# Two weight groups on ScalarE's DMA queue, a third without a throttle, and five groups in the first attention block

## The chip, the cores and the metric

The kernel runs on one core of one Trainium2 chip. Five engines work side by side, each through its own list of instructions in order: TensorE (PE, with its weight loads PEld), VectorE (DVE), ScalarE (ACT), GpSimd (POOL) and SyncE (SP), which here only issues DMAs. A DMA is issued by one engine and carried out by 16 DMA engines. The metric is the device time of one execution in microseconds (us). What is compared is the median of several executions.

## The reference

Causal attention with a decay, then two feed-forward layers, all in float32 with float64 weights:

```
q, k, v: (4, 8, 576, 64)   f: (4, 8, 576)
cum   = cumsum(log(clip(f, 1e-4, 1)))
score = q k^T / 8 + cum[:, None] - cum[None, :]      (masked above the diagonal)
x     = softmax(score) v           -> 2304 tokens of 512
h     = x @ w_in  (512 x 2048);    y = max(0.01 h, h) @ w_out  (2048 x 512)
out   = ((y @ w_a) * (y @ w_b)) @ moe2_w_out         (512 x 1536, twice; 1536 x 512)
```

## The kernel before

**Stages.** Attention runs in blocks `(b, r)`: batch `b`, and of its 576 tokens the first 256 (`r = 0`) or the last 320 (`r = 1`). Eight heads go in four pairs. The first feed-forward layer works on chunks of 256 tokens of x: chunk 0 needs only block (0, 0). The first matmul of chunk 0, `h` at L624, can therefore begin as soon as the last pair of block (0, 0) has given its part of x. From there on the matmuls of the feed-forward layers are woven between those of the later attention blocks, and after attention they run alone.

**One pair of the first block.** q and k are loaded and turned by TensorE (`tqk`), copied to `qn` (ACT) and `kn` (DVE); `s` is the score matmul. GpSimd builds the decay and mask `p` from `cumb`, a row of the cumulative sum broadcast over 128 partitions by a DMA that reads `cum_dram`. VectorE adds `s` to `p` and takes the row minimum (L371), ScalarE exponentiates (L339), VectorE makes the reciprocal `rec`, ScalarE multiplies (L380), TensorE transposes (`pp`), ScalarE copies (`ph`), TensorE multiplies with v (`av`), and x comes out as a high part `xh` (ACT) and a low part `xl` (DVE), which split a float32 in two numbers that TensorE takes at full rate. Two chunks of keys per head pass through this, of 128 and of 256 columns. Many of these carry L76, a wrapper's line, so names tell them apart. Buffers of `p` are two per head of a pair, so that pair 2 waits for the transposes of pair 0.

**Weights.** The weights arrive as float64, and a "group" is 128 columns of w_in and 128 rows of w_out: two DMAs of 512 KB into `raw_a`. There are 16 groups, a_0 to a_15. A conversion takes each to float32 high and low parts: `Abs` on ScalarE (L118), four operations on VectorE (L119, L120, L121, L124), a copy to the high part on ScalarE (L111), and the subtraction for the low part on VectorE (L112). A pair of groups is needed by each of the eight steps of a chunk.

**What sets the order.** A scheduler orders the instructions of each engine ahead of time. Attention's operations carry a priority offset of 300 in the first block, conversions none. `load_next` is called at every ninth step of the first block, and each call also fetches a further group. The fetch of group fi waits for the start of the conversion of group fi - 2 (`behind=begun[fi - 2]`). All loads go through SP in order. The DMAs of all engines share eight completion semaphores in turn (`DMAHW0` to `DMAHW7` in the listings of the program order), so a DMA waits for the landing of the one that had its semaphore before, eight earlier.

Of the kernel before, what the change touches and what calls it, by code (L numbers as in the profile page):

```python
# [13 lines left out]
ALU = mybir.AluOpType  # L14
# [3 lines left out]
P = 128  # L18
# [3 lines left out]
TOP_MIN = 2.0**-15  # L22
TOP_MAX = 122874.0
# [3 lines left out]
def kernel(  # L27
# [30 lines left out]
    wpool = ctx.enter_context(tc.tile_pool(name="wpool", bufs=1))  # L58
# [37 lines left out]
    ORDER = mybir.DependencyInfo(mybir.DependencyClass.NoSync, mybir.DependencyReason.DATA)  # L96
# [9 lines left out]
    def f32(ap):  # L106
        return ap.bitcast(F32)
# [3 lines left out]
        nc.scalar.copy(hi, src)  # L111
        (lo_engine or nc.gpsimd).tensor_tensor(out=lo, in0=src, in1=f32(hi), op=ALU.subtract)  # L112

    def from_double(raw, c):


        top, low, t = raw[:, :, 1], raw[:, :, 0], c.bitcast(F32)
        first = nc.scalar.activation(t, top.bitcast(F32), AF.Abs)  # L118
        nc.vector.tensor_scalar(t, t, TOP_MIN, TOP_MAX, op0=ALU.max, op1=ALU.min)  # L119
        nc.vector.tensor_scalar(c, c, 5, 2, op0=ALU.logical_shift_left, op1=ALU.logical_shift_right)  # L120
        nc.vector.scalar_tensor_tensor(  # L121
            out=c, in0=low, scalar=29, in1=c, op0=ALU.logical_shift_right, op1=ALU.bitwise_or
        )
        nc.vector.scalar_tensor_tensor(  # L124
            out=c, in0=top, scalar=-0x40000000, in1=c, op0=ALU.bitwise_and, op1=ALU.bitwise_or
        )
        return t, first

    begun = []
    SYNC = mybir.DependencyInfo(mybir.DependencyClass.Sync, mybir.DependencyReason.DATA)  # L130

    def fetch_weight(pool, tag, name, *parts, behind=None):

        raw = pool.tile([P, 1024, 2], I32, tag=tag, bufs=1, name=f"raw_{name}")
        for z, src in enumerate(parts):
            view = raw[:, 512 * z : 512 * z + 512, :].rearrange("p n t -> p (n t)")
            if len(src.shape) == 3:
                view = view.rearrange("p (a b) -> p a b", b=2 * P)
            ins = nc.sync.dma_start(view, src)  # L139
            if behind is not None:  # L140
                tc.add_manual_dep(ins.ins, behind.ins.name, SYNC, reason="weights wait for an earlier conversion")
            elif pool is wpool and name == "a_1":
                tc.keep_in_program_order(ins)
        return raw, pool, tag, name

    def convert_weight(tpool, raw, pool, tag, name):

        c = tpool.tile([P, 1024], I32, tag="t", bufs=2, name=f"c_{name}")
        t, first = from_double(raw, c)
        w = pool.tile([P, 2, 1024], F32R, tag=tag, bufs=1, name=f"w_{name}")  # L150
        split(w[:, 0, :], w[:, 1, :], t, nc.vector)
        begun.append(first)
        return w[:, 0, 0:512], w[:, 1, 0:512], w[:, 0, 512:1024], w[:, 1, 512:1024]

    def cols(w, j):

        return w[:, 2 * j * P : 2 * (j + 1) * P].rearrange("(c p) f -> p c f", p=P)

    def rows(w, j):
        return w[j * P : (j + 1) * P, :]  # L160
# [22 lines left out]

    fs = ap_.tile([B * H, S], F32, tag="cumb", bufs=3, name="fs")
    nc.sync.dma_start(fs, f.rearrange("b h s -> (b h) s"))
    nc.vector.tensor_scalar(fs, fs, 0.0001, 1.0, op0=ALU.max, op1=ALU.min)
    nc.scalar.activation(fs, fs, AF.Ln)
    ones = ap_.tile([B * H, S], F32, tag="tk", name="ones")  # L190
    nc.vector.memset(ones, 1.0)
    cum = ap_.tile([B * H, S], F32, tag="cumb", bufs=3, name="cum")
# [23 lines left out]
    def att_scores(b, r, h, st):  # L216
# [15 lines left out]
        if b == 0:  # L232
            if j == 0:

                qn = ap_.tile([P, 384], F32, tag="qhh", bufs=2, name=f"qn_{nm}")
                kn = ap_.tile([P, S], F32, tag="ks", bufs=3, name=f"kn_{nm}")
                xq = ap_.tile([P, 2, 2, 64], F32, tag=("xq", "xq2")[hp % 2], name=f"xq_{nm}")
                full, rest = nk // P, nk % P
                xk = ap_.tile([P, 5, 2, 64], F32, tag=("xk", "xk2")[hp % 2], name=f"xk_{nm}")
                for u in range(2):  # L240
                    nc.sync.dma_start(xq[:, 0:2, u, :], q[b, h + u, q0 : q0 + 2 * P, :].rearrange("(c p) d -> p c d", p=P))
                    if r == 1:
                        nc.sync.dma_start(xk[64:P, 4, u, :], q[b, h + u, q0 + 2 * P : S, :])
                    nc.sync.dma_start(xk[:, :full, u, :], k[b, h + u, : full * P, :].rearrange("(c p) d -> p c d", p=P))
                    if rest:
                        nc.sync.dma_start(xk[:rest, full, u, :], k[b, h + u, full * P : nk, :])
                if first:
                    tqk = ps_y.tile([P, 2, T1], F32, tag="y", bufs=2, name=f"tqk_{nm}")
                    tq = tqk[:, 0, :]
                else:  # L250
                    tq = ps_a.tile([P, 320], F32, tag="ps", bufs=3, name=f"tq_{nm}")
                for c, at, w in ((0, 0, P), (1, P, P), (2, 2 * P, 64))[: 2 + r]:
                    part, sl = (xq[:, c, :, :], slice(0, P)) if c < 2 else (xk[64:P, 4, :, :], slice(64, P))
                    pe_att.transpose(tq[:, at : at + w], part.rearrange("p u d -> p (u d)"), ident[sl, sl])
                act_att.mul(qn[:, :nq], tq[:, :nq], -SCALE)
                for c0, c1 in ((0, 2), (2, 5))[: 1 + r]:
# [163 lines left out]
                yield  # L420

    def evac(hi, lo, src):
        act_att.copy(hi, src)
        return dve_att.tensor_tensor(out=lo, in0=src, in1=f32(hi), op=ALU.subtract)


    def att_values(b, r, h, st):
# [7 lines left out]
        if j == 0:  # L435
            full, rest = nk // P, nk % P
            if b == 0:
                vs = ap_.tile([P, 5, 2, 64], F32, tag=("vs", "vhl")[hp % 2], name=f"vn_{nm}")
            else:
                vs = ap_.tile([P, 5, 2, 64], F32, tag="vs", name=f"vs_{nm}")  # L440
            for u in range(2):
                nc.sync.dma_start(vs[:, :full, u, :], v[b, h + u, : full * P, :].rearrange("(c p) d -> p c d", p=P))
                if rest:
                    nc.sync.dma_start(vs[:rest, full, u, :], v[b, h + u, full * P : nk, :])
            if b == 0:
                vhls[pair] = vs
# [39 lines left out]
        if b == 0:  # L486
# [16 lines left out]
                    if kt == u == 0:  # L503
                        tc.add_manual_dep(made.ins, st["second"].ins.name, SYNC, reason="both heads at once")
            ch, cl = x_chunk(tok0 // T1)
            low = evac(ch[:, hp, :], cl[:, hp, :], av)
            if r == 0:
                dve_held.first = low
            yield
            return  # L510
        av = ps_a.tile([P, 256], F32, tag="ps", bufs=3, name=f"av_{nm}")
# [86 lines left out]
    blocks = [(b, r) for b in range(B) for r in range(2)]  # L598
    wa = {}

    landing = []

    def fetch_a():
        fi = len(landing)
        if fi < NF1:
            landing.append(fetch_weight(wpool, f"w{fi}", f"a_{fi}", cols(w_in, fi), rows(w_out, fi), behind=begun[fi - 2] if fi > 1 else None))

    def load_a(fi):
        if fi == 0:
            fetch_a()  # L610
        wa[fi] = convert_weight(stage, *landing[fi])

    def l1(i, pr):
        ch, cl = x_chunk(i)
# [198 lines left out]
    def load_next():  # L813
        nonlocal loaded
        if loaded < NF1:
            load_a(loaded)
            loaded += 1
            fetch_a()

    for s, _ in enumerate(att_steps(0)):  # L820
        if s == 0:
            fetch_a()
        if s % 9 == 8:
            load_next()
    for engine in (act_att, dve_att, pool_att):
        engine.offset = 0
# [103 lines left out]
```

## Time and profile before

| | |
|---|---|
| median of 3 runs (lowest to highest) | 1086.86 us (1086.01 to 1087.88) |
| the profiled execution | 1085.58 us |
| its span, first to last instruction | 1083.8 us |
| mean granted TensorE clock | 0.987 of full speed |
| busy PE, PEld | 1050.4 us (97%), 943.7 us (87%) |
| busy DVE, ACT, POOL | 588.3 us (54%), 549.2 us (51%), 210.4 us (19%) |
| share of PE in the chain that ended last | 89% |

The profiled execution is 1.78 us longer than its span, and 1.28 us below the median. In the page's table of 40 slices, 27.1 us each, PE is busy 3 tenths of the first slice, 6 of the second and 9 of nearly every later one. The averages hide that the engines have different limits in different stretches: VectorE and ScalarE are busy 5 to 9 tenths in the first half and 1 to 2 tenths at the end.

### The profile page before, as it was taken

To read this page: it belongs to the slowest core of one execution; us is meant where nothing else is said; L and a number is where in the kernel's file an instruction comes from. 1 tells how busy PE (TensorE), PEld (TensorE's weight loads), DVE (VectorE), ACT (ScalarE), POOL (GpSimd) and SP (SyncE) were. 2 spreads that over 40 slices of the span, in tenths; PEclk is the share of its full clock that TensorE was granted. 3 is DMA by queue.
4 is the path that set the end of the run, shared out by engine and by line. 5 is a ranking of instruction groups with operands and counts; after the bars stand their busy time and mean duration, and the time that the engine had idled before them with its cause. 6 is when DMAs were issued, how large, how long until landed. Compare 5 with 4: busy or idle time off the path is not lost.

```text
span 1083.8 us, 19124 instructions
## 1 busy us (share of the span) xinstructions
PE 1050.4 (97%) x6941; PEld 943.7 (87%) x6941; DVE 588.3 (54%) x1314; ACT 549.2 (51%) x1221; POOL 210.4 (19%) x434
## 2 busy tenths in 40 slices
PE   3699999999999999999999999999999999999998
PEld 1378789999999999999999998888888888888897
DVE  5899758878787778666439798112112111212122
ACT  5877778877787878677435554112112111211121
POOL 2623524343244324223000001001002000100000
PEclk9689999999999999999999999999999999999999
DMA  8886245333552244321234761102001000100010
GB/s 237 241 261 188 42 88 100 77 91 66 104 107 63 64 86 107 70 47 42 79 98 158 232 233 31 29 1 78 1 1 45 24 1 1 49 0 1 1 40 20
DMA packets 185726, 86.74 MB, mean 80 GB/s; under 512 B 143840, under 2 KB 173536, under 8 KB 185632
## 3 DMA queue, kind: packets, MB, share of 16 engines
q1 hardware_dynamic: 180736, 80.80, 28.5%
q10 hardware_dynamic: 4896, 4.72, 1.3%
q8 instruction: 55, 0.90, 0.3%
q14 instruction: 39, 0.32, 0.1%
HBM read 75.96 MB, written 9.51 MB: 79 GB/s over the span
## 4 chain that ended last, share of the span: by engine, by line
PE 89%; DMA 4%; issue 2%; ACT 2%; DVE 2%; SPq 1%; POOL 1%; POOLq 0%; ACTq 0%; DVEq 0%
PE ab L722 27%; PE y L653 17%; PE h L624 17%; PE o L745 14%; PE s L76 5%; PE av L76 5%; PE pp L76 4%; DMA raw_a<-in_moe_w_out_dram 1%; DMA cumb<-cum_dram 1%; DMA raw_a<-in_moe_w_in_dram 1%; DMA y_dram<-yo 0%; PE tk L76 0%; ACT p L380 0%; SPq L139 0%; POOL p L361 0%
## 5 line engine op out<-in xcount | busy, mean ns | idle before, releaser
L722 PE MATMUL ab<-yh,w_ab 128*128 128x512 f32 (+1 forms) x960 | 279.6, 367 | 0.0
L624 PE MATMUL h<-xh,w_a 128*128 128x256 f32 x1152 | 227.7, 284 | 0.5 <-ACT hs L636 0.3
L653 PE MATMUL y<-gh,w_a 128*128 128x256 f32 x1152 | 225.4, 282 | 0.0
L722 PEld LDWEIGHTS ab<-yh,w_ab 128*128 128x128 f32 x960 | 174.1, 188 | 30.4
L728 DVE TENSOR_TENSOR p<-ab,p 128x512 f32<-128x512 f32 (+1 forms) x60 | 38.3, 638 | 283.3 <-PE ab L722 283.3
L624 PEld LDWEIGHTS h<-xh,w_a 128*128 128x128 f32 x1152 | 185.6, 190 | 3.9 <-issue 1.3
L653 PEld LDWEIGHTS y<-gh,w_a 128*128 128x128 f32 x1152 | 183.3, 188 | 3.6 <-issue 2.4
L722 PE MATMUL ab<-yl,w_ab 128*128 128x512 f32 (+1 forms) x480 | 176.2, 367 | 0.0
L624 PE MATMUL h<-xl,w_a 128*128 128x256 f32 x576 | 163.6, 284 | 0.0
L653 PE MATMUL y<-gl,w_a 128*128 128x256 f32 x576 | 160.6, 281 | 0.0
L745 PE MATMUL o<-w_c,pph 128*128 128x512 f32 x432 | 142.6, 389 | 0.0
L727 ACT COPY p<-ab 128x512 f32<-128x512 f32 (+1 forms) x60 | 32.7, 544 | 172.7 <-PE ab L722 172.7
L361 POOL TENSOR_SCALAR p<-cumb,ncum_t 128x384 f32<-128x384 f32 (+1 forms) x112 | 82.1, 741 | 144.6 <-PE pp L76 70.2
L624 PEld LDWEIGHTS h<-xl,w_a 128*128 128x128 f32 x576 | 109.5, 190 | 0.3
L653 PEld LDWEIGHTS y<-gl,w_a 128*128 128x128 f32 x576 | 108.3, 188 | 0.7 <-issue 0.4
L722 PEld LDWEIGHTS ab<-yl,w_ab 128*128 128x128 f32 x480 | 90.1, 188 | 15.3
L111 ACT CAST pph<-p 128x512 fp32r<-128x512 f32 (+1 forms) x60 | 34.6, 577 | 128.8 <-DVE p L728 128.5
L745 PEld LDWEIGHTS o<-w_c,pph 128*128 128x128 f32 x432 | 81.1, 188 | 16.6
L112 POOL TENSOR_TENSOR yl<-sy,yh 128x512 fp32r<-128x512 f32 (+1 forms) x16 | 19.9, 1254 | 389.3 <-ACT yh L111 389.2
L339 ACT ACTIVATE p<-p,stat 128x384 f32<-128x384 f32 (+4 forms) x128 | 76.9, 602 | 29.6 <-DVE stat L371 23.9
L745 PE MATMUL o<-w_c,ppl 128*128 128x512 f32 x216 | 84.2, 390 | 0.0
L638 DVE TENSOR_TENSOR gl<-hs,gh 128x512 fp32r<-128x512 f32 x72 | 50.6, 702 | 38.4 <-ACT hs L636 37.8
(143 smaller groups left out, 1695.2 us busy)
## 6 DMA issues: line engine op xcount, KB each, us to landing
cumb<-cum_dram SPq DMA_DIRECT2D x32, 288.0 KB, 4.0
raw_a<-in_moe_w_in_dram SPq DMA_DIRECT2D x16, 512.0 KB, 5.4
raw_a<-in_moe_w_out_dram SPq DMA_DIRECT2D x16, 512.0 KB, 6.5
raw_ab<-in_moe_w_a_dram SPq DMA_DIRECT2D x12, 512.0 KB, 5.2
raw_ab<-in_moe_w_b_dram SPq DMA_DIRECT2D x12, 512.0 KB, 6.7
raw_c<-in_moe_w_out_dram SPq DMA_DIRECT2D x12, 512.0 KB, 5.1
xq<-in_q_dram SPq DMA_DIRECT2D x144, 32.0 KB, 2.0
y_dram<-yo ACTq DMA_DIRECT2D x18, 256.0 KB, 2.8
```

The lines of the kernel that those rows point to most:

```text
L76: return method(*args, **kw)
L111: nc.scalar.copy(hi, src)
L112: (lo_engine or nc.gpsimd).tensor_tensor(out=lo, in0=src, in1=f32(hi), op=ALU.subtract)
L339: act_att.activation(pt, pt, AF.Exp, bias=stat[:, 0, s : s + 1], scale=-1.0, accum_out=stat[:, 1, s : s + 1])
L361: pool_att.tensor_scalar(pt, cumb[:, :n], 1.0, ncum_t[:, t, bh : bh + 1], op0=ALU.mult, op1=ALU.add)
L624: made = nc.tensor.matmul(hps[:, u, :], w[:, c * P : c * P + P], x[:, c, :], start=(n == 0), stop=(n == 3 * ND - 1))
L638: nc.vector.tensor_tensor(out=gl, in0=hs, in1=f32(gh), op=ALU.subtract)
L653: nc.tensor.matmul(o, w[:, d * P : d * P + P], g[:, u, :], start=(fi == 0 and n == 0 and d % 2 == 0), stop=(fi == NF1 - 1 and n == 2 and d ...
L722: nc.tensor.matmul(o[:, :tn], w[:, c * P : c * P + P], y[:, c, :tn], start=(m == 0), stop=(m == 3 * ND - 1))
L727: nc.scalar.copy(p[:, :tn], ab[0][:, :tn])
L728: nc.vector.tensor_tensor(out=p[:, :tn], in0=ab[1][:, :tn], in1=p[:, :tn], op=ALU.mult)
L745: nc.tensor.matmul(o, g[:, t * P : t * P + P], w, start=(fi == 0 and m == 0), stop=(fi == NF2 - 1 and m == 2))
```

## The change

Groups a_0 and a_1 are loaded from ScalarE's queue (`engine=nc.scalar`), the first at the very start. Group a_2 is no longer held behind a conversion. The first loads on SP are put in a fixed order (`in_line`): q and k of the first two pairs, then a_2, then v of the first pair, as far as the calls come in that order. `load_next` is called at steps 0, 5, 9, 26 and 44 of the first block, so five groups belong to it. Groups from a_5 on are held (`held=True`): their `Abs` and their first operation on VectorE come, in the order of their engines, behind the copy `xh` and the subtraction `xl` of the first block's last x. That is an order on the same engine and not a semaphore.

```diff
+    first_x = []
-    def from_double(raw, c):
+    def from_double(raw, c, held):
         first = nc.scalar.activation(t, top.bitcast(F32), AF.Abs)
-        nc.vector.tensor_scalar(t, t, TOP_MIN, TOP_MAX, op0=ALU.max, op1=ALU.min)
+        clamp = nc.vector.tensor_scalar(t, t, TOP_MIN, TOP_MAX, op0=ALU.max, op1=ALU.min)
+        if held:
+            for made, x in zip((first, clamp), first_x):
+                tc.add_manual_dep(made.ins, x.ins.name, ORDER, reason="weights behind the first block's last x")
...
+    line = []
+    def in_line(made, early):
+        if early:
+            if line:
+                tc.add_manual_dep(made.ins, line[-1].ins.name, ORDER, reason="order of the first loads")
+            line.append(made)
...
-            ins = nc.sync.dma_start(view, src)
+            ins = (engine or nc.sync).dma_start(view, src)
+            in_line(ins, early)
             if behind is not None:
                 tc.add_manual_dep(ins.ins, behind.ins.name, SYNC, reason="weights wait for an earlier conversion")
-            elif pool is wpool and name == "a_1":
-                tc.keep_in_program_order(ins)
...
+    landing = []
+    def fetch_a():
+        fi = len(landing)
+        if fi < NF1:
+            landing.append(
+                fetch_weight(
+                    wpool, f"w{fi}", f"a_{fi}", cols(w_in, fi), rows(w_out, fi),
+                    behind=begun[fi - 2] if fi > 2 else None, engine=nc.scalar if fi < 2 else None, early=fi == 2,
+                )
+            )
+    fetch_a()
     fs = ap_.tile([B * H, S], F32, tag="cumb", bufs=3, name="fs")
     nc.sync.dma_start(fs, f.rearrange("b h s -> (b h) s"))
     nc.vector.tensor_scalar(fs, fs, 0.0001, 1.0, op0=ALU.max, op1=ALU.min)
     nc.scalar.activation(fs, fs, AF.Ln)
+    fetch_a()
...
-            low = evac(ch[:, hp, :], cl[:, hp, :], av)
+            ends = evac(ch[:, hp, :], cl[:, hp, :], av)
             if r == 0:
-                dve_held.first = low
+                first_x[:] = ends
+                dve_held.first = ends[1]
...
-        wa[fi] = convert_weight(stage, *landing[fi])
+        wa[fi] = convert_weight(stage, *landing[fi], held=fi >= 5)
...
+            if 2 < len(landing) < loaded + 2:
+                fetch_a()
...
     for s, _ in enumerate(att_steps(0)):
-        if s == 0:
+        if s == 4:
             fetch_a()
-        if s % 9 == 8:
+        if s in (0,5,9,26,44):
             load_next()
```

What this does to the order of the engines shows at three places. First ScalarE, in the first block, around the exponential of pair 0's second chunk (`p_0_0`, 128x256); `c_a<-raw_a` is the `Abs` of a group. Before:

```order
L118 ACTIVATE c_a_303<-raw_a_198 128x1024
L76 ACTIVATE p_0_0_127,stat_0_0_108<-p_0_0_127,stat_0_0_108 128x256
L76 ACTIVATE qn_0_4_231<-tqk_0_4_239 128x256
L76 ACTIVATE p_0_1_139,stat_0_0_108<-p_0_1_139,stat_0_0_108 128x256
L111 CAST w_a_257<-c_a_251 128x1024
L76 ACTIVATE p_0_2_206,stat_0_2_147<-p_0_2_206,stat_0_2_147 128x128
L76 ACTIVATE p_0_3_218,stat_0_2_147<-p_0_3_218,stat_0_2_147 128x128
L76 ACTIVATE p_0_0_127<-p_0_0_127,rec_0_0_0_181 128x128
```

And after, where `raw_a_203` is group a_3 and `raw_a_227` is a_4:

```order
L120 ACTIVATE c_a_315<-raw_a_203 128x1024
L111 CAST w_a_224<-c_a_218 128x1024
L76 ACTIVATE p_0_1_151,stat_0_0_114<-p_0_1_151,stat_0_0_114 128x128
L76 ACTIVATE qn_0_4_255<-tqk_0_4_263 128x256
L120 ACTIVATE c_a_419<-raw_a_227 128x1024
L76 ACTIVATE p_0_0_133,stat_0_0_114<-p_0_0_133,stat_0_0_114 128x256
L76 ACTIVATE p_0_1_151,stat_0_0_114<-p_0_1_151,stat_0_0_114 128x256
L111 CAST w_a_321<-c_a_315 128x1024
L76 ACTIVATE p_0_2_230,stat_0_2_159<-p_0_2_230,stat_0_2_159 128x128
L76 ACTIVATE p_0_3_242,stat_0_2_159<-p_0_3_242,stat_0_2_159 128x128
L76 ACTIVATE p_0_0_133<-p_0_0_133,rec_0_0_0_208 128x128
```

Before, the third group's `Abs` (a_2) stood ahead of that exponential; now the fourth's and the fifth's stand ahead of it, and one `qn` copy has left the stretch behind it.

Second SP at the program's start, after the change, with the semaphores that each waits for; `DMAHW0`, `3`, `5` and `7` belong to the four loads that ScalarE issues:

```order
L213 DMA fs<-in_f_dram 32x576
L269 DMA xq_0_0_117<-in_q_dram 128x2x64
L272 DMA xk_0_0_118<-in_k_dram 128x2x64
L269 DMA xq_0_0_117<-in_q_dram 128x2x64
L272 DMA xk_0_0_118<-in_k_dram 128x2x64 [waits DMAHW0_49]
L269 DMA xq_0_2_162<-in_q_dram 128x2x64 [waits DMAHW1_49]
L221 DMA cum_dram<-cum 32x576 [waits DMAHW2_49,DVE_49]
L272 DMA xk_0_2_163<-in_k_dram 128x2x64 [waits DMAHW3_49]
L269 DMA xq_0_2_162<-in_q_dram 128x2x64 [waits DMAHW4_49]
L272 DMA xk_0_2_163<-in_k_dram 128x2x64 [waits DMAHW5_49]
L153 DMA raw_a_186<-in_moe_w_in_dram 128x4x256 [waits DMAHW6_49]
L153 DMA raw_a_186<-in_moe_w_out_dram 128x1024 [waits DMAHW7_49]
```

The second half of the first pair's k, and all of SP's list behind it, now waits for the landing of a_0's first half, and a_2's second half for that of a_1's.

Third VectorE at the end of the first block, where `xl<-av_0_7` is the last x. Before:

```order
L121 SCALAR_TENSOR_TENSOR c_a_462<-raw_a_377,c_a_462 128x1024
L76 TENSOR_TENSOR xl_289<-av_0_5_480,xh_288 128x256
L124 SCALAR_TENSOR_TENSOR c_a_462<-raw_a_377,c_a_462 128x1024
L119 TENSOR_SCALAR c_a_507<-c_a_507 128x1024
L120 TENSOR_SCALAR c_a_507<-c_a_507 128x1024
L112 TENSOR_TENSOR w_a_468<-c_a_462,w_a_468 128x1024
L121 SCALAR_TENSOR_TENSOR c_a_507<-raw_a_428,c_a_507 128x1024
L76 TENSOR_TENSOR xl_289<-av_0_7_525,xh_288 128x256
```

After:

```order
L76 TENSOR_TENSOR xl_301<-av_0_3_392,xh_300 128x256
L76 TENSOR_SCALAR rec_0_6_0_476<-stat_0_6_351 128x2
L76 RECIPROCAL rec_0_6_0_476<-rec_0_6_0_476 128x2
L76 TENSOR_SCALAR rec_0_7_2_481<-stat_0_6_351 128x2
L76 RECIPROCAL rec_0_7_2_481<-rec_0_7_2_481 128x2
L76 TENSOR_TENSOR xl_301<-av_0_5_468,xh_300 128x256
L76 TENSOR_TENSOR xl_301<-av_0_7_501,xh_300 128x256
L121 TENSOR_SCALAR c_a_692<-c_a_692 128x1024
```

All of group a_5 and three operations of a_6 stood ahead of the last x, and now a_5 begins behind it. On TensorE the score matmul `s_1_0_2` of the second block, which stood ahead of the first `h`, now stands behind that step's 24 matmuls.

## Rows read from the trace of the kernel before

**Rows 1.** Busy time by engine (count), granted clock, DMA share, GB/s, by stretch

```profile
0.00:10.00 10.00, 3.29 (x15) 1.92 (x15) 3.06 (x5) 3.99 (x7) 0.71 (x6) 1.00 0.67 190
10.00:20.00 10.00, 2.07 (x7) 0.79 (x6) 5.99 (x11) 4.73 (x8) 7.34 (x16) 1.00 0.88 269
20.00:30.00 10.00, 5.96 (x24) 3.53 (x24) 9.93 (x26) 8.01 (x19) 1.71 (x3) 1.00 0.92 256
35.00:62.00 27.00, 19.19 (x81) 12.79 (x82) 24.42 (x50) 19.92 (x44) 17.76 (x22) 0.50 0.92 267
50.00:60.00 10.00, 9.45 (x39) 6.24 (x38) 9.57 (x15) 7.57 (x16) 7.38 (x8) 0.50 1.05 312
57.00:1075.00 1018.00, 1016.86 (x6794) 923.84 (x6792) 543.85 (x1219) 509.19 (x1132) 180.94 (x385) 1.00 0.27 71
```

**Rows 2.** Chain of waits: start, us, what; the first two steps of h

```profile
57.22 5.23 PE h L624 x24
65.01 2.80 PE h L624 x24
```

**Rows 3.** Timeline of PE: start, us, what, [idle before <-releaser]

```profile
27.25 1.57 PE L76 MATMUL pp<-ident,p 128*128 128x128 f32 x6 [0.71 <-ACT p L76]
...
43.64 1.54 PE L76 MATMUL pp<-ident,p 128*128 128x128 f32 x6
...
49.64 1.52 PE L76 MATMUL pp<-ident,p 128*128 128x128 f32 x6 [1.12 <-ACT p L76]
...
52.54 1.60 PE L76 MATMUL av<-ph,vn 128*64 128x256 f32 x8
...
55.57 1.65 PE L76 MATMUL s<-kn,qn 64*128 64x384 f32 x4 [0.52 <-ACT kn L265]
...
127.09 0.28 PE L624 MATMUL h<-xh,w_a 128*128 128x256 f32 x1
```

**Rows 4.** Timeline of ACT and POOL in the first block

```profile
21.32 1.21 ACT L118 ACTIVATE c_a<-raw_a 128x1024 f32<-128x1024 f32 x1 [1.38 <-DMA raw_a<-in_moe_w_out_dram]
22.71 0.51 ACT L76 ACTIVATE p<-p,stat 128x256 f32<-128x256 f32 x1 [0.18 <-DVE stat L76]
...
12.14 1.97 POOL L76 TENSOR_SCALAR p<-cumb,ncum_t 128x128 f32<-128x128 f32 x2 [10.82 <-DMA cumb<-cum_dram]
```

**Rows 5.** Timeline of DVE: around the last x, and the last conversion's end

```profile
55.44 1.21 DVE L121 SCALAR_TENSOR_TENSOR c_a<-raw_a,c_a 128x1024 int32<-128x1024 int32 x1
56.57 0.41 DVE L76 TENSOR_TENSOR xl<-av,xh 128x256 fp32r<-128x256 f32 x1
...
123.73 1.23 DVE L112 TENSOR_TENSOR w_a<-c_a,w_a 128x1024 fp32r<-128x1024 f32 x1
```

**Rows 6.** A conversion's operations until 58 us: count, busy, mean ns, idle before

```profile
L118 ACT ACTIVATE c_a<-raw_a 128x1024 f32<-128x1024 f32 x8 | 9.3, 1162 | 6.2 <-DMA raw_a<-in_moe_w_out_dram 5.6 <-DVE w_a L112 0.5
L121 DVE SCALAR_TENSOR_TENSOR c_a<-raw_a,c_a 128x1024 int32<-128x1024 int32 x7 | 8.6, 1233 | 0.1
L112 DVE TENSOR_TENSOR w_a<-c_a,w_a 128x1024 fp32r<-128x1024 f32 x6 | 7.7, 1276 | 0.0
L124 DVE SCALAR_TENSOR_TENSOR c_a<-raw_a,c_a 128x1024 int32<-128x1024 int32 x6 | 7.3, 1220 | 0.0
L111 ACT CAST w_a<-c_a 128x1024 fp32r<-128x1024 f32 x6 | 6.3, 1047 | 4.0 <-DVE c_a L124 3.9
L120 DVE TENSOR_SCALAR c_a<-c_a 128x1024 int32<-128x1024 int32 x7 | 5.1, 724 | 0.1
L119 DVE TENSOR_SCALAR c_a<-c_a 128x1024 f32<-128x1024 f32 x7 | 4.9, 702 | 3.6 <-ACT c_a L118 3.6
```

**Rows 7.** DMA issues until 58 us: count, KB each, median us to landing

```profile
raw_a<-in_moe_w_in_dram SPq DMA_DIRECT2D x9, 512.0 KB, 6.0
...
cumb<-cum_dram SPq DMA_DIRECT2D x8, 128.0 KB, 5.0
xq<-in_q_dram SPq DMA_DIRECT2D x14, 64.0 KB, 4.8
```

More of the change, by code (lines that the diff above doesn't have):

```diff
@@ L130, with fetch_weight @@
     SYNC = mybir.DependencyInfo(mybir.DependencyClass.Sync, mybir.DependencyReason.DATA)
-    def fetch_weight(pool, tag, name, *parts, behind=None):
+    line = []
[4 more added lines that the diff above has]
+            line.append(made)
+    def fetch_weight(pool, tag, name, *parts, behind=None, engine=None, early=False):
         raw = pool.tile([P, 1024, 2], I32, tag=tag, bufs=1, name=f"raw_{name}")
@@ L138, in fetch_weight, with convert_weight @@
                 view = view.rearrange("p (a b) -> p a b", b=2 * P)
-            ins = nc.sync.dma_start(view, src)
+            ins = (engine or nc.sync).dma_start(view, src)
+            in_line(ins, early)
             if behind is not None:
                 tc.add_manual_dep(ins.ins, behind.ins.name, SYNC, reason="weights wait for an earlier conversion")
-            elif pool is wpool and name == "a_1":
-                tc.keep_in_program_order(ins)
         return raw, pool, tag, name
-    def convert_weight(tpool, raw, pool, tag, name):
+    def convert_weight(tpool, raw, pool, tag, name, held=False):
         c = tpool.tile([P, 1024], I32, tag="t", bufs=2, name=f"c_{name}")
-        t, first = from_double(raw, c)
+        t, first = from_double(raw, c, held)
         w = pool.tile([P, 2, 1024], F32R, tag=tag, bufs=1, name=f"w_{name}")
@@ L240, in att_scores @@
                 for u in range(2):
-                    nc.sync.dma_start(xq[:, 0:2, u, :], q[b, h + u, q0 : q0 + 2 * P, :].rearrange("(c p) d -> p c d", p=P))
+                    early = r == 0 and hp < 2
+                    in_line(nc.sync.dma_start(xq[:, 0:2, u, :], q[b, h + u, q0 : q0 + 2 * P, :].rearrange("(c p) d -> p c d", p=P)), early)
                     if r == 1:
                         nc.sync.dma_start(xk[64:P, 4, u, :], q[b, h + u, q0 + 2 * P : S, :])
-                    nc.sync.dma_start(xk[:, :full, u, :], k[b, h + u, : full * P, :].rearrange("(c p) d -> p c d", p=P))
+                    in_line(nc.sync.dma_start(xk[:, :full, u, :], k[b, h + u, : full * P, :].rearrange("(c p) d -> p c d", p=P)), early)
                     if rest:
@@ L422, in evac @@
     def evac(hi, lo, src):
-        act_att.copy(hi, src)
-        return dve_att.tensor_tensor(out=lo, in0=src, in1=f32(hi), op=ALU.subtract)
+        high = act_att.copy(hi, src)
+        return high, dve_att.tensor_tensor(out=lo, in0=src, in1=f32(hi), op=ALU.subtract)
     def att_values(b, r, h, st):
@@ L441, in att_values @@
             for u in range(2):
-                nc.sync.dma_start(vs[:, :full, u, :], v[b, h + u, : full * P, :].rearrange("(c p) d -> p c d", p=P))
+                in_line(
+                    nc.sync.dma_start(vs[:, :full, u, :], v[b, h + u, : full * P, :].rearrange("(c p) d -> p c d", p=P)),
+                    (b, r, hp) == (0, 0, 0),
+                )
                 if rest:
@@ L599 @@
     wa = {}
[L601 to L606, printed above, removed]
     def load_a(fi):
-        if fi == 0:
-            fetch_a()
-        wa[fi] = convert_weight(stage, *landing[fi])
+        wa[fi] = convert_weight(stage, *landing[fi], held=fi >= 5)
     def l1(i, pr):
@@ L817, in load_next @@
             loaded += 1
+            if 2 < len(landing) < loaded + 2:
+                fetch_a()
+    for s, _ in enumerate(att_steps(0)):
+        if s == 4:
             fetch_a()
-    for s, _ in enumerate(att_steps(0)):
-        if s == 0:
-            fetch_a()
-        if s % 9 == 8:
+        if s in (0,5,9,26,44):
             load_next()
```

## The prediction

> **What bounds the kernel now.** I read the busy times by stretch first. From 57 us to 1075 us TensorE is busy 1016.86 of 1018.00 us at the full granted clock (2.4 GHz), so nothing can be won there without fewer matmuls, and the change takes none away [rows 1]. Before 57 us TensorE is mostly idle: 3.29, 2.07 and 5.96 us busy in the first three stretches of ten. So the time of the kernel is the time at which the first feed-forward matmul `h` starts, plus a length that stays as long as TensorE never starves again. The chain of waits has that start at 57.2 us [rows 2]. The timeline of TensorE then shows the first attention block as a pipeline of four pairs of heads; the transposes `pp` of pairs 0, 2 and 3 begin at 27.25, 43.64 and 49.64 us [rows 3]. That is 22.4 us for three steps, 7.5 us each. VectorE explains the pace: it is busy 9.93 of 10 us between 20 and 30 us and 24.42 of 27 between 35 and 62 us [rows 1], and most of this is not attention. One conversion costs it 0.70 + 0.72 + 1.23 + 1.22 + 1.28 = 5.15 us, and costs ScalarE 1.16 + 1.05 = 2.2 us [rows 6]. I therefore price four things: where the pipeline starts, its pace, its tail, and what is handed on to the stretch behind 57 us.
>
> **1. The pipeline starts later.** In the order of ScalarE the exponential of pair 0's second chunk now stands behind the `Abs` of the fifth group, a_4, and not of the third, a_2. Before, that third `Abs` began at 21.32 us, released by its DMA, and the exponential at 22.71 us [rows 4]. So I need the landing of a_4. Ahead of it in the queues lie ten halves of 512 KB, six broadcasts of 128 KB and some eighteen loads of about 64 KB [rows 7]: 5.24 + 0.79 + 1.18 = 7.2 MB. In the trace 1.90 + 2.69 + 2.56 = 7.15 MB moved in the first 30 us, and the first ten moved at only 190 GB/s with the DMA engines 0.67 busy [rows 1]. Those ten held small loads and one group that was issued behind them. Now ScalarE issues a group at once, beside SP's small loads. I let the first ten move at the rate of the second ten, 269 GB/s: 5.4 MB by 20 us, and 1.8 MB more at 256 GB/s, which is 27.1 us. `Abs` takes 1.16 us: 28.3 us. From the exponential to `pp` of pair 0 it was 27.25 - 22.71 = 4.5 us; one `qn` copy has left that stretch and VectorE has less to do in it, so I take 4.1: `pp` at 32.4 us, 5.1 us later than before. Bounds: at the best ten-us rate of these rows, 312 GB/s, from 2 us on, a_4 lands at 25.1, 2.0 us sooner; at the rates as they stood, at 30.2, 3.1 us later.
>
> Two delays lie under this cover. SP now waits for a_0's first half before the second half of the first k, and every later load of SP is behind that wait, with the broadcasts for GpSimd at the end of the list. GpSimd began at 12.14 us when the first broadcast landed [rows 4]; I expect about 15 to 16 us, behind three groups. It must have pair 0's second head ready before the exponential at 28.3 us, so some 8 us of cover are left. If the broadcasts came as late as a_4, that cover would be gone and the start would move one for one.
>
> The Trainium skill (DMA: Bandwidth & Descriptors, section "Issuing engines are not separate DMA queues") speaks against this step: transfers from SP's and ScalarE's queues run on the same 16 engines and interleave, and a second issuing engine saves only the time to issue. The trace agrees as far as it goes, with the DMA engines 0.88 and 0.92 busy between 10 and 30 us [rows 1]; it leaves the first ten open. By the rule a_4 lands at the rates as they stood, 3.1 us later than I take; that is the first rival below.
>
> **2. The pace.** Only the copies and remaining operations of a_3 and a_4 fall in the three steps from `pp` of pair 0 on; after them attention has VectorE to itself. The shortest step before, from 43.64 to 49.64 us, took 6.0 us [rows 3] and still carried about one conversion, of which ScalarE's part was 2.2 us [rows 6]. So a step lies between 6.0 - 2.2 = 3.8 us, where ScalarE alone sets it, and 6.0 us, where the chain from one engine to the next does. I take 5.3, nearer the upper end, since attention's own chain is unchanged and TensorE still runs it at half clock: three steps are 15.9 instead of 22.4 us, and `pp` of pair 3 is at 48.3 us.
>
> **3. The tail.** Before, `pp` of pair 3 began at 49.64 us and `av` ended at 52.54 + 1.60 = 54.1 us [rows 3], 4.5 us later. But `xl` began only at 56.57, behind a conversion's operation at 55.44 us [rows 5], and `h` started at 57.2, also behind a score matmul of the second block of 1.65 us [rows 3]. Now no conversion stands ahead of `xl` and that matmul stands behind `h`. The 4.5 us stay, then come the copy `xh` and `xl`, each about 0.41 us with a hand-over: 0.9 us. So `h` starts at 48.3 + 5.4 = 53.7 us, 3.5 us sooner than 57.2.
>
> **4. What is handed on.** The score matmul is paid behind `h` instead: 1.65 us at half clock, 0.8 at full. I take 0.8 us, with 1.65 as the other end. The clock: between 35 and 62 us the granted clock was 0.50 (1.2 GHz) [rows 1], and the first 24 matmuls of `h` took 5.23 us against 2.80 for the next [rows 2]. TensorE was sparse before the clock fell and dense for the last 12 us before it rose; the end of the block is as dense after the change, so I price no difference. If the clock came back before `h` this would give 2.4 us, if it came back a step later it would cost 2.6.
>
> VectorE gets a debt. Before, a_5 and three operations of a_6 were done ahead of the last x: 5.15 + 0.70 + 0.72 + 1.23 = 7.8 us that now lie behind it. Before, the last conversion ended at 123.73 + 1.23 = 125.0 us [rows 5], and TensorE reached the first matmul of that group (the 181st `h` matmul) at 127.09 us [rows 3]: 2.1 us of margin. Taken as they stood, the lists would have TensorE wait 7.8 - 2.1 = 5.7 us. But the order of TensorE is new as well. The listing has that group's first `h` 22 rows later, with attention's matmuls of later blocks ahead of it, which is other work for TensorE during the debt. These rows need VectorE too, so I leave 0.3 us of waiting; the ends are 0 and 5.7. Fetching a_7 and later groups waits for a held `Abs`, which is hidden: VectorE has about 10 us of a_5, a_6 and attention before it needs a_7, and a group's halves land 6 us after their issue [rows 7].
>
> **Sum.** -3.5 + 0.8 + 0.3 = -2.4 us on the profiled execution's 1085.58 us (span 1083.8 and 1.78 around it): 1083.2. The median of the runs is 1.28 us above that execution, so I predict 1084.5 us.
>
> **Rivals.**
>
> *The bytes bind.* The second queue adds no rate, a_4 lands at 30.2 us and everything behind it moves by 3.1 us: 1087.6 us. For it speaks the 0.92 of busy DMA engines; against it that the first ten us had a third of them free, and that two of the five groups no longer queue behind small loads.
>
> *The debt binds.* VectorE and not TensorE sets the stretch up to the last conversion: TensorE waits at the later groups, from a_10 on, for 5.7 us instead of 0.3: 1084.5 + 5.4 = 1089.9 us. It decides against the change once these waits pass 0.3 + 2.4 = 2.7 us, and visibly so from 4.9. For it speaks that the margin was only 2.1 us; against it the new filler. This is the case that is slower.
>
> *ScalarE alone sets the pace.* Steps of 3.8 us: 4.5 us less over three, 1080.0 us; half of that is likelier than all. For it speaks how much of VectorE falls free; against it that a step crosses four engines.
>
> *It does nothing* beyond reordering, because the first x is bound by the chain of pair 0 alone: steps as before, with only the tail's gain against the late start, would be 1086.9 - 2.1 + 5.1 + 0.8 = 1090.7 us. The busy 24.42 of 27 us of VectorE [rows 1] speak against it.
>
> **Chances.** The forecast's own case, 1083 to 1086 us, has 0.50. The bytes have 0.20, ScalarE's pace 0.16 (1080 to 1082.5), the debt 0.10, nothing gained in pace 0.04. A measurement of this kernel can tell about 0.2%, 2.2 us, from no change, and my forecast lies just beyond that. Of the 0.50 I put 0.31 on faster and 0.19 on the same; ScalarE's pace is faster; of the bytes 0.19 is the same and 0.01 slower; the other two are slower. So 0.47 faster, 0.38 the same, 0.15 slower. The range takes in the fast pace almost to its end and the late bytes, and leaves out most of the debt: 1080.5 to 1088.5 us.
>
> **What would show it.** Step 1: `Abs` of a_4 begins at 25 to 30 us, released by a DMA, and the exponential of pair 0's second chunk right behind it. Step 2: three steps of `pp` together 14 to 18 us, VectorE with gaps between 35 and 50 us. Step 3: `xl` of the last pair within 0.3 us of `xh`'s end, and the first `h` at 52 to 56 us. Step 4: TensorE idle less than 2 us in all from there to 140 us, and from then on as before. The forecast fails if `h` starts later than 56 us or if TensorE waits for VectorE's low parts for more than 3 us.

## The result, and the profile after

| | before | after |
|---|---|---|
| median of 6 runs (lowest to highest) | 1085.62 us (1084.60 to 1087.88) | 1092.19 us (1091.44 to 1094.76) |
| the profiled execution, its span | 1085.58 us, 1083.8 us | 1092.96 us, 1091.2 us |
| first `h` of chunk 0, of chunk 1 in it | 57.15 us, 147.53 us | 55.43 us, 153.41 us |

The ratio is 1.0061, 95% interval 1.0051 to 1.0071: 6.6 us slower, where I had forecast 2.4 us faster.

The start did come earlier. The timeline of TensorE (start, us, what; answers to [rows 3]):

```profile
34.82 1.56 PE L76 MATMUL pp<-ident,p 128*128 128x128 f32 x6 [0.38 <-ACT p L76]
...
41.67 1.52 PE L76 MATMUL pp<-ident,p 128*128 128x128 f32 x6
...
46.90 1.54 PE L76 MATMUL pp<-ident,p 128*128 128x128 f32 x6
...
50.71 1.54 PE L76 MATMUL pp<-ident,p 128*128 128x128 f32 x6
...
53.53 0.97 PE L76 MATMUL av<-ph,vn 128*64 128x256 f32 x8
54.43 0.64 PE L76 MATMUL tk<-ident,xk 128*128 128x128 f32 x3
55.43 0.39 PE L647 MATMUL h<-xh,w_a 128*128 128x256 f32 x1 [0.36 <-DVE xl L76]
...
140.64 0.36 PE L647 MATMUL h<-xh,w_a 128*128 128x256 f32 x1
...
153.41 0.28 PE L647 MATMUL h<-xh,w_a 128*128 128x256 f32 x1
```

`h` starts at 55.43 and not 57.15 us. But the 181st `h` matmul, which reads the last weight group and ran at 127.09 us [rows 3], comes at 140.64, and the first `h` of chunk 1 at 153.41, 5.9 us later than before. The loss lies between. Busy time by stretch (columns as in [rows 1]), after:

```profile
40.00:55.40 15.40, 13.49 (x62) 8.15 (x62) 7.02 (x29) 12.44 (x39) 7.83 (x21) 0.56 0.50 117
55.43:153.41 97.98, 94.06 (x650) 73.69 (x651) 85.65 (x175) 73.75 (x149) 33.70 (x50) 0.97 0.52 148
90.00:141.00 51.00, 47.08 (x307) 34.68 (x304) 46.67 (x94) 38.55 (x78) 23.92 (x33) 0.93 0.44 122
128.88:135.70 6.82, 6.62 (x30) 4.92 (x30) 6.12 (x13) 2.27 (x7) 0.33 (x1) 0.50 0.24 39
```

and the same stretches before:

```profile
40.00:55.40 15.40, 9.62 (x40) 5.68 (x40) 14.31 (x28) 12.45 (x30) 13.31 (x17) 0.50 0.96 289
57.15:147.53 90.38, 90.38 (x644) 72.88 (x643) 75.44 (x156) 68.35 (x137) 33.26 (x52) 0.97 0.52 144
90.00:141.00 51.00, 51.00 (x370) 40.72 (x369) 40.31 (x87) 39.23 (x81) 21.23 (x33) 1.00 0.35 89
```

The third number is VectorE. From 40 to 55.4 us it worked 14.31 us before and works 7.02 now: it stands idle for 8.4 us while the held groups wait, and has that work behind `h`. From 90 to 141 us it is busy for 46.67 us and not 40.31, and TensorE, which had no idle time there, gets through 307 matmuls and not 370. What TensorE waits for, in its timeline:

```profile
109.94 0.50 PE L676 MATMUL y<-gh,w_a 128*128 128x256 f32 x2 [0.89 <-ACT gh L658]
...
111.02 1.13 PE L76 MATMUL s<-kn,qn 64*128 64x512 f32 x4 [0.58 <-DVE stat L90]
...
126.87 0.92 PE L76 MATMUL s<-kn,qn 64*128 64x384 f32 x4 [0.47 <-DVE stat L90]
128.93 0.80 PE L676 MATMUL y<-gh,w_a 128*128 128x256 f32 x2 [1.14 <-ACT gh L658]
...
160.63 0.38 PE L647 MATMUL h<-xh,w_a 128*128 128x256 f32 x1 [1.50 <-ACT hs L659]
```

They name scores' minima (`stat`) and the two copies between `h` and `y`, not low parts; the chain of waits shows what stands behind them (start, us, what):

```profile
120.59 0.72 DVE c_a L125
121.31 1.14 DVE w_a L112
122.45 0.02 issue
122.48 1.19 ACT c_a L120
...
129.08 1.24 DVE w_a L112
130.32 0.04 issue
130.36 2.50 PE h L647 x10
```

From 111 to 130 us the chain stays on VectorE but for one `Abs` on ScalarE, and most of its time there goes into conversions (`c_a`, `w_a`); a low part releases `h` at 130.36 us. Before, the chain is TensorE alone from 84 to 131 us.

The account of the profiled executions, 7.4 us: the first `h` 1.7 sooner; its first 24 matmuls 3.08 us instead of 5.23 [rows 2], 2.15 less; the score matmul behind it, 0.8 more; TensorE idle 3.92 (97.98 - 94.06); half clock from 128.88 to 135.70 us, 6.62 us busy, of which half, 3.3, is lost; the wait of 1.50 at 160.63. That is 5.7; the other 1.7 us lie in time in which TensorE counts as busy, and I can't assign them. No conversion stands in the chain from 150 to 160 us: what the 1.50 us waited for is attention's work of the second block on VectorE and ScalarE.

### The profile page after: what moved, and what is told of

Read it like the earlier page. It is cut to its first block, busy times and chain, and to the rows that moved or that the text cites. A ratio compares the mean times of both kernels' runs of the same rounds, so it can differ in the third digit from the quotient of the medians.

```text
span 1091.2 us, 19103 instructions
## 1 busy us (share of the span) xinstructions
PE 1051.2 (96%) x6941; PEld 943.8 (86%) x6941; DVE 588.6 (54%) x1314; ACT 548.4 (50%) x1221; POOL 205.0 (19%) x434
## 4 chain that ended last, share of the span: by engine, by line
PE 88%; DVE 3%; DMA 2%; ACT 1%; issue 1%; SPq 0%; POOL 0%; DVEq 0%; POOLq 0%; ACTq 0%
PE ab L745 27%; PE y L676 17%; PE h L647 17%; PE o L768 13%; PE av L76 5%; PE s L76 5%; PE pp L76 3%; DMA cumb<-cum_dram 1%; DMA xk<-in_k_dram 1%; DVE w_a L112 0%; DVE c_a L129 0%; DVE p L90 0%; ACT p L76 0%; DVE c_a L125 0%; SPq L334 0%
## 5 line engine op out<-in xcount | busy, mean ns | idle before, releaser
L389 POOL TENSOR_SCALAR p<-cumb,ncum_t 128x384 f32<-128x384 f32 (+1 forms) x112 | 75.1, 678 | 148.1 <-PE pp L76 58.5
```

The source lines that it names most:

```text
L389: pool_att.tensor_scalar(pt, cumb[:, :n], 1.0, ncum_t[:, t, bh : bh + 1], op0=ALU.mult, op1=ALU.add)
```

## The experiments

All ratios are to the kernel before on the same chip. "Ahead" is how many of VectorE's operations on weight groups stand ahead of the last x in its order. The times of `h` are those of each run's profiled execution, PE the matmuls from 90 to 141 us, "to the end" the span less the first `h`. The profiled execution of e4 is 3.8 us above the median of its runs. A left-out operation or a hold also gives TensorE a new order of matmuls; where it bears on the reading I say so.

| run | ahead | first `h`, chunk 0 | chunk 1 | PE | span | to the end | ratio (95%) |
|---|---|---|---|---|---|---|---|
| before | 33 | 57.15 | 147.53 | 370 | 1083.8 | 1026.7 | |
| after | 25 | 55.43 | 153.41 | 307 | 1091.2 | 1035.8 | 1.0061 (1.0051 to 1.0071) |
| e1 | 25 | 53.15 | 149.93 | 340 | 1086.3 | 1033.2 | 1.0028 (1.0017 to 1.0038) |
| e2 | 43 | 64.56 | 157.27 | 370 | 1091.2 | 1026.6 | 1.0077 (1.0064 to 1.0089) |
| e3 | 30 | 57.39 | 151.62 | 366 | 1086.2 | 1028.8 | 1.0033 (1.0022 to 1.0044) |
| e4 | 25 | 61.90 | 160.23 | 316 | 1096.4 | 1034.5 | 1.0099 (1.0082 to 1.0116) |
| e5 | 48 | 69.96 | 163.48 | 364 | 1097.5 | 1027.5 | 1.0122 (1.0108 to 1.0135) |
| e6 | 30 | 60.18 | 155.14 | 377 | 1090.5 | 1030.3 | 1.0060 (1.0046 to 1.0073) |
| e7 | 30 | 58.85 | 152.88 | 364 | 1089.2 | 1030.4 | 1.0049 (1.0036 to 1.0062) |
| e8 | 25 | 55.69 | 163.80 | 256 | 1101.0 | 1045.3 | 1.0146 (1.0132 to 1.0160) |
| e9 | 25 | 55.94 | 153.41 | 311 | 1090.9 | 1035.0 | 1.0062 (1.0049 to 1.0074) |
| e10 | 30 | 58.92 | 156.00 | 366 | 1092.3 | 1033.4 | 1.0062 (1.0048 to 1.0076) |
| e11 | 30 | 57.27 | 148.50 | 372 | 1088.5 | 1031.2 | 1.0046 (1.0033 to 1.0058) |
| e12 | 25 | 55.41 | 153.62 | 362 | 1088.0 | 1032.6 | 1.0018 (1.0005 to 1.0031) |

**e1, one operation less per held conversion.**

```diff
-        nc.vector.scalar_tensor_tensor(out=c, in0=low, scalar=29, in1=c, ...)
+        if not held: nc.vector.scalar_tensor_tensor(out=c, in0=low, scalar=29, in1=c, ...)
```

> The changed kernel with one of VectorE's five operations of a conversion left out for the held groups a_5 to a_15 (the 1.22 us one that shifts in the low word, so the weights lose their low bits): 11 x 1.2 = 13 us less work on VectorE behind the last x, nothing else changed but the order that follows from it. Theory (VectorE's debt): TensorE loses about 10 us between 90 and 141 us because low parts come late, and the half clock at 129 us is a consequence of those waits; so 8 to 10 us come back, 1082 to 1085 us, with no half clock behind 57 us. Rival (TensorE's order): the matmuls were put in an order in which they wait for later attention, however much VectorE has to do; so under 2 us come back, 1090 to 1092 us.

1087.67 us: by the ratios 3.6 us of the 6.6 come back, between the two theories. (The medians differ by 4.5 us, but the kernel before was 0.6 us faster beside e1.) The chain of waits of this run passes through conversions only up to 97 us; from 99 to 137 us it is TensorE alone, here its end:

```profile
123.78 1.30 PE s L76 x4
125.08 0.91 PE y L676 x6
126.00 0.89 PE av L76 x8
...
133.83 1.67 PE av L76 x16
135.49 0.69 PE pp L76 x5
136.19 1.08 PE s L76 x4
137.27 0.02 issue
137.30 0.69 DVE p L90
```

So conversions no longer stop TensorE there. But TensorE's order of matmuls is another as well, from 74 us on, so the run doesn't tell how much of this is the shorter list of VectorE. What is left at the end of the chain is attention's second block, and the granted clock was 0.50 again, from 142.94 to 146.35 us, against the theory. In the profiled execution 2.3 us of the gain is an earlier first `h`, of which the last section speaks; from the first `h` to the end only 2.6 us of 9.1 came back.

**e2, no hold.** `held=fi >= 5` becomes `held=False`.

> The changed kernel without the hold: groups a_5 and later are again placed ahead of the last x where the order lets them. Theory (VectorE's debt): VectorE fills the 8 us that it stood idle between 40 and 55 us, the first h comes later, at 56 to 59 us instead of 55.4, and the waits up to 141 us go: 1083 to 1088 us. Rival (late start): the second queue and the fixed order of loads made pair 0 of the first block 7.6 us later, and that is what is paid; then this kernel is no better than the changed one, 1090 to 1094 us.

1093.01 us, in the rival's range and for its reason. `pp` of pair 0 begins at 34.85 us, 7.6 us later than before, and that of pair 3 at 57.20: the three steps take 22.4 us and the tail 7.4, both as before, so the first `h` comes 7.4 us later. My theory had the waits right (370 matmuls from 90 to 141 us, as before) and the start wrong by 5.6 us: 18 more operations stand ahead of the last x, VectorE is idle no more, and the gain in pace is gone. The hold is worth 9.1 us at the start and costs as much behind it: the length from the first `h` to the end is 1026.6 us here, as before, and 1035.8 with the hold, which is the only edit between the two.

**e3, six groups.**

```diff
-        if s in (0,5,9,26,44):
+        if s in (0,5,9,26,35,44):
-        wa[fi] = convert_weight(stage, *landing[fi], held=fi >= 5)
+        wa[fi] = convert_weight(stage, *landing[fi], held=fi >= 6)
```

> The changed kernel with a sixth call of load_next in the first block (at step 35) and groups held from a_6 on. Theory (VectorE's debt): one conversion, 5.2 us of VectorE, moves from behind the last x into its idle time between 40 and 55 us; TensorE gets back 4 to 6 us and the half clock at 129 us may go with it: 1085.5 to 1088.5 us, the first h within 1 us of 55.4. Rival (TensorE's order): 1090 to 1093 us.

1088.24 us, at the upper end of the theory's range, though its first `h` was to stay within 1 us of 55.4 and came 2.0 us later. One conversion moved into VectorE's idle time costs the first `h` those 2.0 us and gives TensorE its 366 matmuls back:

```profile
90.00:141.00 51.00, 50.90 (x366) 39.06 (x364) 43.68 (x93) 38.95 (x82) 20.99 (x35) 1.00 0.40 111
```

**e4, SP's queue.** `engine=nc.scalar if fi < 2 else None` becomes `engine=None`.

> The changed kernel with a_0 and a_1 on SP's queue again (order of the loads and hold as changed). Theory (VectorE's debt): the queue only moves the start of pair 0, by less than 2 us either way; the debt stays: 1090 to 1094 us. Rival (late start, the queue itself is the cost): the first cumb broadcast lands at 12 to 14 us instead of 17.4, the first h at 52 to 54 us: 1086 to 1089 us.

1094.44 us, just above the theory's range: the queue is not the cost. But it moves the start by far more than the 2 us that I had allowed: `pp` of pair 0 began at 41.62 us, 6.8 us later. Without ScalarE's queue the same order of loads is worse: the first broadcast lands at 22.55 us instead of 17.41, the first `h` comes at 61.90.

**e5, the loads alone.** As e2, and `if s % 9 == 8` for the calls again.

> The loads of the changed kernel (a_0 and a_1 on ScalarE's queue from the start, a_2 unthrottled, fixed order) with the old calls of load_next at every ninth step and no hold. Theory (the bytes come in the wrong order): weights that land first push back fs, q, k and the broadcasts, attention's first pair starts about 5 us later and nothing makes up for it: first h at 60 to 64 us, 1088 to 1092 us. Rival (the loads help, only calls and hold cost): first h at 55 to 57 us, 1083 to 1086 us.

1099.38 us, worse than either theory: the loads alone cost 13 us. `pp` of pair 0 starts at 32.30 us, which is earlier than after, but the pairs then take 9 to 10 us each (42.56, 51.54): 48 operations of conversions stand ahead of the last x. The late start is not where the time goes. From the first `h` to the end it is 1027.5 us, again as before.

**e6 and e7, loads in another order.** Both are e3 with ScalarE's four loads behind its `Ln`; e7 has a_2 behind the first two pairs' broadcasts as well, and q, k and v out of the fixed order.

```diff
+            if engine: tc.add_manual_dep(ins.ins, ln.ins.name, ORDER, reason="behind Ln")
```

> The kernel with six groups, with ScalarE's four loads of a_0 and a_1 put behind its Ln instead of ahead of it. Theory (the bytes come in the wrong order): fs, q and k land as in the kernel before (first q at 3.0 and not 6.6 us), the first broadcast at 14 to 16 us and not 17.3, pp of pair 0 at 32 to 34 us, first h at 54.5 to 56.5 us and not 57.4: 1085.5 to 1087.5 us. Rival (pair 0 waits for the conversions of a_2 to a_4 and not for its own loads): pp of pair 0 stays at 34.5 to 36 us, 1088 to 1090 us.

> As the run with the loads behind Ln, and a_2 behind the broadcasts of the first two pairs instead of ahead of them. Theory (the bytes come in the wrong order): first broadcast at 12 to 13.5 us, pp of pair 0 at 29 to 32 us, first h at 52 to 55 us, 1082.5 to 1085.5 us. Rival (VectorE's total work binds in the end): h is as early, but VectorE has as much left behind it and TensorE waits for low parts between 90 and 141 us again: 1087 to 1090 us.

1093.17 and 1091.40 us: above both ranges. The theory wasn't put to the test, because the broadcasts didn't come sooner. The first q did land at 3.1 and 3.0 us, but the broadcasts only at 17.99 and 16.90. They were issued at 14.32 and 13.83, behind a load of k that went out 0.06 and 0.01 us after the landing of a_1 on ScalarE's queue (13.84 and 13.41), with which SP's list shares its semaphores. e7 had `pp` of pair 0 at 33.13 us, 1.8 us sooner than e3, and the last pair at 53.74: the start was lost again within the block.

**e8, the low part on GpSimd.**

```diff
-        split(w[:, 0, :], w[:, 1, :], t, nc.vector)
+        split(w[:, 0, :], w[:, 1, :], t, nc.gpsimd if held else nc.vector)
```

> The changed kernel with the subtraction for the low part of the held groups a_5 to a_15 on GpSimd instead of VectorE: 11 x 1.2 = 13 us of VectorE become about 11 x 2.5 = 27 us of GpSimd (estimated from its 1.25 us for half that width), which has 70 us free between 55 and 160 us. Theory (VectorE's debt): the waits up to 141 us shrink by 8 to 10 us, as in the run that left an operation out: 1083 to 1088 us. Rival (a slower engine in the chain): the low parts come later or the masks p are held up on GpSimd, 1092 us or more.

1101.97 us, in the rival's range, but not by what the rival names alone: VectorE's own operations became longer. One operation of VectorE and the subtraction on GpSimd beside it:

```profile
81.47 2.53 DVE L125 TENSOR_SCALAR c_a<-c_a 128x1024 int32<-128x1024 int32 x1
...
81.04 2.40 POOL L112 TENSOR_TENSOR w_a<-c_a,w_a 128x1024 fp32r<-128x1024 f32 x1
```

The operation of VectorE ends 0.56 us after GpSimd's, and alone it takes 0.69. Its mean from 55 to 145 us rose from 0.708 to 1.538 us. The Trainium skill (SBUF — State Buffer, section "SBUF: two separate sides") says that the two engines share a pair of ports; of an operation of GpSimd and one of VectorE in a two-port mode or with two inputs in SBUF, the one that starts first holds the pair for the whole instruction while the other is blocked. The two rows above agree; in which mode VectorE's operation ran no row shows.

**e9, the calls and the hold on the old loads; e10, the same with six groups.** The kernel before with `first_x`, `held=fi >= 5` and the calls at 0, 5, 9, 26, 44; in e10 with `held=fi >= 6` and 35 as a sixth.

> The kernel before with the five early calls of load_next and the hold from a_5 on, and all loads as before (SP's queue, throttled, no fixed order). Theory (VectorE's debt): the first h comes at 52 to 56 us, and TensorE loses 6 to 10 us up to 141 us waiting for low parts: 1088 to 1092 us, as the whole change. Rival (the new loads cost it): without them the start is early enough and TensorE waits for less: 1082 to 1086 us.

> As the run with early calls and hold on the old loads, but with a sixth call at step 35 and the hold from a_6 on. Theory (VectorE's debt): one conversion more ahead of the last x, the first h about 2 us later than with five, the waits up to 141 us nearly gone: 1084 to 1088 us. Rival (the new loads cost it): with the old loads and few waits 1081 to 1084 us.

e9: 1092.68 us, 0.7 us above the theory's range, and the whole loss of the change without any of its loads:

```profile
90.00:141.00 51.00, 46.45 (x311) 33.90 (x308) 47.22 (x95) 39.05 (x78) 24.26 (x33) 0.97 0.47 126
```

So calls and hold are enough for the whole loss, and the new loads add nothing to it. TensorE's order is also nearly that of after: 6910 of 6941 matmuls stand in the same place. The parts don't add up, though: the loads alone cost 13 us (e5), and with six groups the new loads are the better ones (e3 against e10). e10, 1093.51 us, missed both ranges: as in e3 the waits up to 141 us are gone, but the first `h` is 1.5 us later than there, and the granted clock was 0.50 for 10.24 us from 145.22 us on.

**e11, only a_6 held.** The kernel before with `if s % 9 == 8 and loaded < 6` and `held=fi >= 6`.

> The kernel before with its old loads and its old times of calls, but without the seventh call in the first block, and held from a_6 on: only three operations of a_6 (0.70 + 0.72 + 1.23 = 2.65 us) and its Abs move behind the last x. Theory (VectorE's debt, with 2.1 us of margin at the last group): first h at 55 to 56.5 us, and of the 2.65 us behind it most is covered: 1084 to 1086.5 us, no loss and little gain. Rival (any work put behind the last x comes back one for one): 1086 to 1089 us.

1091.34 us, above both ranges. The first `h` was no earlier (57.27), so nothing was won, and chunk 1 was 1.0 us later. From 90 to 141 us TensorE had no idle time (372 matmuls), from 141 to 300 us it was idle for 4.1 us, where the kernel before has 0.9; its order had changed too, from 74 us on. Why these gaps arose I didn't follow. So 2.65 us of held work cost more than itself, though TensorE didn't wait up to 141 us.

**e12, two operations less.** As e1, with the operation that puts in the sign and the top bit left out as well.

> The changed kernel with two of VectorE's five operations of a conversion left out for the held groups (the two of 1.22 us that put the low word and the sign in, so their weights are wrong): 11 x 2.4 = 27 us less on VectorE behind the last x, twice as much as in the run that left one out and gave back 4.5 us. Theory (VectorE's debt alone): the waits behind the first h go altogether and 5 to 9 us more come back than the 4.5: 1079 to 1083 us. Rival (TensorE's order): what was left after the first 13 us lies in attention's own chain of the second block, between 140 and 160 us and later, and stays: 1086 to 1089 us, little better than with one operation left out.

1088.02 us, the rival's range: a second 13 us of VectorE's work gave nothing that the runs can tell from e1. Stretches of this run, the second from the last `y` of chunk 0 to the first `h` of chunk 1:

```profile
90.00:141.00 51.00, 51.00 (x362) 39.20 (x360) 28.96 (x76) 35.68 (x79) 18.25 (x34) 1.00 0.35 94
138.15:153.62 15.47, 14.68 (x69) 10.00 (x68) 10.53 (x41) 12.52 (x34) 3.34 (x9) 0.67 0.27 53
142.63:152.87 10.24, 10.18 (x42) 6.96 (x41) 6.87 (x28) 8.43 (x24) 3.26 (x9) 0.50 0.26 48
```

and the second of them before:

```profile
139.07:147.53 8.46, 8.46 (x60) 5.77 (x59) 3.38 (x14) 6.07 (x15) 2.84 (x9) 1.00 0.30 75
```

From 90 to 141 us TensorE no longer waits and VectorE is idle for 22 of 51 us, and still chunk 1 begins at 153.62 us. In both kernels only attention is left behind the last `y` of chunk 0. It takes 7.0 us longer here, and 5.1 of them are the granted clock, which was 0.50 for 10.24 us.

None of the twelve was faster than the kernel before.

## Why the prediction was wrong

*What bounds the kernel.* I wrote that the time is the start of the first `h` plus a length that stays. The table bears that out only where no conversion is held: the length is 1026.7 us before, 1026.6 in e2 and 1027.5 in e5, though the first `h` starts at 57.15, 64.56 and 69.96 us. With the hold from a_6 on it is 1028.8 to 1033.4 us, with the hold from a_5 on and VectorE's full work 1034.5 to 1035.8. It grows as "ahead" falls from 33 to 30 and 25. Most of the difference lies ahead of chunk 1: from the first `h` of chunk 0 to that of chunk 1 it took 90.4 us before, 98.0 after, and 91 to 108 in the runs. The span minus the first `h` of chunk 1 is 936.3 us before, 937.8 after, and 934 to 938 in all runs but e11 (940.0). The rows that I rested on showed TensorE without idle time in both parts and could not tell them apart; VectorE's 543.85 us [rows 1] could have been cut at 147 us.

*Step 1* was late by more than I said, 7.6 us and not 5.1. a_4 landed at 27.94 us (27.1), its `Abs` began at 28.65 (28.3), but the exponential only at 30.28, and `pp` at 34.82 (32.4). The cover under which I hid GpSimd's late start was not there:

```profile
17.60 4.65 POOL L76 TENSOR_SCALAR p<-cumb,ncum_t 128x128 f32<-128x128 f32 x4 [16.28 <-DMA cumb<-cum_dram]
...
30.28 0.51 ACT L76 ACTIVATE p<-p,stat 128x256 f32<-128x256 f32 x1 [0.49 <-DVE stat L76]
```

The broadcast came at 17.4 and not at 15 to 16 us, GpSimd's masks held up the first two exponentials, and the second chunk's waited for VectorE's row minimum, not for `Abs`. The bytes did not bind: the first ten us moved 259 GB/s.

*Step 2* was right in its sum: 50.71 - 34.82 = 15.9 us for three steps, as forecast. That is in part luck, for the steps took 6.9, 5.2 and 3.8 us where I had 5.3 for each, and the first lies above the 6.0 that I gave as the upper end. *Step 3* took 4.7 us, not 5.4, with `av` at full clock. So `h` started at 55.4 and not 53.7 us.

*Step 4* is the one that failed: what the hold hands on was priced at 0.8 us for the score matmul and 0.3 us for the debt, and cost 9.1 us from the first `h` to the end (1035.8 and not 1026.7). That the hold does it is shown by e2, which differs from after by the hold alone and has 1026.6; e9 shows calls and hold on the old loads to be enough for it (1035.0). Of the 9.8 us between my -2.4 and the +7.4 of the profiled executions 8.0 are this step, and 1.8 the first `h`. In the trace of after these are 3.9 us of waits up to 141 us, 1.5 us at 160.63 us, 3.3 us of half clock, the score matmul's 0.8 us and 1.7 us that I can't assign, less the 2.15 us that the clock gave back at the first `h`, which I had named but not priced. I had let other matmuls of TensorE cover all but 0.3 us of the debt, with 5.7 as the upper end. The filler was itself attention of later blocks, which needs VectorE for every score. I had written this down and priced it at 0.3.

One of my two signs of failure was that TensorE waits for VectorE's low parts for more than 3 us. It was idle for 3.9 us, but a low part ended only 0.14 us of that directly; the others were scores and the copies of chunk 0 behind VectorE's conversions. The rival "the debt binds" (1089.9 us, a chance of 0.10) named the sign and a mechanism that the trace shows up to 141 us; its price was 2.3 us short.

How the hold costs 9.1 us is shown in part only. With VectorE's work cut by 13 and 27 us (e1, e12) 2.6 and 3.2 us of the 9.1 came back, although in e12 no conversion stops TensorE any more from 90 to 141 us. e11 lost 4.6 us from the first `h` to the end with 2.65 us held and no wait of TensorE up to 141 us. So the waits for VectorE are one part. Another is attention's second block just ahead of chunk 1, where e12 lost 5.1 us to the half clock. The clock alone isn't it either: in e7 it was 1.00 from the first `h` on,

```profile
58.85:152.88 94.03, 91.80 (x654) 72.31 (x654) 82.99 (x176) 72.32 (x152) 38.28 (x50) 1.00 0.51 142
```

and the stretch to chunk 1 still took 94.0 and not 90.4 us, with 2.2 us of idle time and 12 more score matmuls in it. What the new order of TensorE costs by itself stays open, because no run gave VectorE less to do and kept that order.

## What to carry to other kernels

When a start is moved forward, look for the next point that other engines must reach, and measure the kernel's length from the start and from there, in runs that switch one part of the change. Work that leaves the path of one engine is not gone: count all that this engine has to do up to that point, and count filler only where it doesn't use the same engine. An engine that a change leaves idle while work for it lies ready is the first sign of a debt. And where a scheduler orders the lists anew, an experiment that takes work away changes the order too.

## What the runs showed of the hardware

The granted clock of a row says nothing of the start of a program. The trace has records of the clock only from 31.36 us on before, from 36.72 after and from 43.95 in e1, and a row shows 1.00 where there is none. The matmuls there go at the lower level's pace, in all fourteen profiles: six `pp` took 1.57 us at 27.25 us, without a record, and 1.54 at 43.64 us, where the granted clock is 0.50 [rows 3]. In e1 they went from 1.52 to 0.88 us within the block, where its records begin, with 1.00:

```profile
41.75 1.52 PE L76 MATMUL pp<-ident,p 128*128 128x128 f32 x6
46.20 0.88 PE L76 MATMUL pp<-ident,p 128*128 128x128 f32 x6
```

So the level rose in the middle of the block there, and its first `h` came 2.3 us sooner than after, with TensorE's order the same up to that point. The mean granted clock of an execution counts the time without a record as 1.00 too: executions of the kernel before with a mean of 0.987 to 0.989 and with 0.998 to 1.000 took the same time, 1083.8 to 1088.2 and 1084.2 to 1088.3 us.

The clock fell to 0.50 at 128.88 us after, behind waits of 0.33, 0.47 and 1.14 us within 4 us. In the kernel before it was 1.00 there [rows 1]. That the waits made it fall isn't shown: in e12 it fell at 142.63 us behind one wait of 0.73 us, and in e6 and e7 it stayed at 1.00 behind waits of 0.73 and 1.02 us within 6 us.
